# Two chained MLPs behind an attention recurrence: weight conversion as a six-stage pipeline, second MLP's weights held in SBUF

## Chip, core and metric

One core of one Trainium2 chip. The metric is the device time of one launch in microseconds, median of several runs. The trace shows one more execution, taken with the hardware profiler.

## What is computed

```python
def _attn_ref(r, k, v, w, a, b):          # each [4, 8, 768, 40], float32
    state = np.zeros((B, H, D, D))
    for t in range(S):
        y[:, :, t] = np.einsum('bhd,bhde->bhe', rt, state)
        Sa = np.einsum('bhde,bhe->bhd', state, at)
        state = state * wt[:, :, None, :] - np.einsum('bhd,bhe->bhde', Sa, bt) \
              + np.einsum('bhd,bhe->bhde', vt, kt)
    return y

x = y.transpose(0, 2, 1, 3).reshape(3072, 320)
x = np.maximum(x @ moe_w_in, 0.0) ** 2 @ moe_w_out            # [320, 2048], [2048, 320]
h = x @ moe2_w_in
out = (h * np.clip(h + 3.0, 0.0, 6.0) / 6.0) @ moe2_w_out
```

The MLP weights reach the kernel as float64. A float64 is two 32-bit words to the kernel, so each weight has to be put together as a float32 from them, and then split into a high part that TensorE's fp32r format holds exactly and a low part, the rest. Products are taken as high x high, high x low and low x high.

## The kernel before

The attention runs in 48 **slots**, one for a chunk of 64 steps of one of four batches. A slot's order is the string ORDER (ORDER0 until the first MLP has inputs), each word a step; four of its words are M. At an M the program calls `fill`, which emits one **piece** of MLP work if there is one (`Moe.piece`) or else a few matmuls that keep TensorE busy, then five steps of a triangular inverse and, with them, steps of the weight conversion (`cstep`). The scheduler is off (`manual_schedule`), so each engine runs its instructions in the order in which this code emits them.

An MLP has 16 blocks f of 128 hidden units. Tokens go in six **groups** of 512. An in-piece (`project_in`) makes a block's hidden values, an out-piece (`out1`, `out2`) adds the block to the output in PSUM. So a group is 32 pieces. A group's inputs are loaded when the attention has written them, every eight slots; the last group of the first MLP and all of the second come after the loop.

`convert` is a generator that turns weights from float64 bits into parts. A **part** is one block of w_in (384 columns) or of w_out (320), in the order two of w_in, two of w_out; 32 parts make an MLP. For each part it emits: load of the bits on SP (L94), Abs of the high word on ScalarE (L126, or L138), scaling of the low word on ScalarE (L130), mask and shift on VectorE (L127), join on VectorE (L135), add of the words on GpSimd (L139), a select that zeroes the smallest on VectorE (L146), a cast to the high part on ScalarE (L70, L74, L75), the subtraction that leaves the low part (L156, GpSimd for w_in, VectorE for w_out), and a store of the low part to DRAM (L78). `finish` holds the last four and is emitted after the next part's first steps.

High parts stay in SBUF. Low parts are read again from DRAM, two blocks at a time, whenever a group needs them (`pair`, L169, on ScalarE's DMA queue), into the rotating buffers wi and wo of the pool m_rot, or m_l2 in the second MLP. In the first MLP the first 16 parts are converted in the slots before the first group (`need(raw1, n_early)` after slot 7); from block 8 on (`direct`) a part is converted straight into the buffer from which the first group reads it, and is held until in-piece f - 2 has been emitted. In the second MLP all parts are direct and held like that, with two steps after each piece. After the loop, four loads of bits and the inputs of the second MLP's first two groups are put on SP's queue at once (L993 to L996).

Of the kernel before, what the change touches and what calls it, by code (L numbers as in the profile page):

```python
# [24 lines left out]
DM = 320  # L25
# [8 lines left out]
class Moe:  # L34


    def __init__(self, tc, ctx, pctx, consts):
# [7 lines left out]
        self.pso4, self.gpool, self.depth = None, self.rot, 2  # L45
# [3 lines left out]
        self.pairs = {}  # L49
# [4 lines left out]
    def weights(self, pool, dram, second, rot):  # L54


        w = {"second": second, "rot": rot, "in": pool.tile([128, NF, 3, 128], F32R, name="wi_hi"),
             "out": pool.tile([128, NF, DM if second else 256], F32R, name="wo_hi")}
        w["li"], w["lo"] = ([dram.tile([128, 2, 384], FP32, name=f"{n}{second}_{k}") for k in range(NF // 2)]
                            for n in ("LI", "LO"))  # L60
        return w

    def split(self, w, part, f, raw, t):

        nc = self.nc
        n = 384
        if part == 0 or w["second"]:
            n = DM if part else 384
            hi = w["out"][:, f] if part else w["in"][:, f].rearrange("p k c -> p (k c)")
            nc.scalar.copy(out=hi, in_=raw)  # L70
            self.low(t[:, 0:n], raw, hi, nc.vector if part else nc.gpsimd)
        else:
            hi = w["out"][:, f]
            nc.scalar.copy(out=hi, in_=raw[:, 0:256])  # L74
            nc.scalar.copy(out=t[:, 0:64], in_=raw[:, 256:320])  # L75
            self.low(t[:, 128:384], raw[:, 0:256], hi, nc.vector)
            self.low(t[:, 64:128], raw[:, 256:320], t[:, 0:64], nc.vector)
        (nc.sync if part else nc.gpsimd).dma_start(out=w["lo" if part else "li"][f // 2][:, f % 2, 0:n], in_=t.bitcast(FP32)[:, 0:n])  # L78

    def convert(self, w, w_in, w_out, scratch, first, direct):  # L80

        nc = self.nc
        self.raw = w
        self.converted = 0
        todo = deque()
        order = [(f, part) for q in range(0, NF, 2) for part in range(2) for f in (q, q + 1)]

        def load(k):
            f, part = order[k]
            bits = scratch(k, 0)[:, 0:640 if part else 768]
            nc.sync.dma_start(out=bits, in_=(w_out if part else w_in)[f])  # L94
            return bits.rearrange("p (c w) -> p c w", w=2)

        count = [0, 0]

        def fill():

            while count[0] < len(order) and count[0] - count[1] < scratch(count[0], 2):
                todo.append(load(count[0]))
                count[0] += 1

        fill()
        yield
        late = []
        for k, (f, part) in enumerate(order):
            n = DM if part else 384
            if f >= direct and f % 2 == 0:  # L110

                while (self.n_out if part else self.n_in) < first + f - 2:
                    if late:
                        late.pop()()
                    yield "held"
                self.pairs[w["second"], part, f] = w["rot"].tile([128, 2, 384], F32R, tag=("wi", "wo")[part], name="wd")
            own = scratch(k, 3)
            fill()
            bits = todo.popleft()
            low, high = bits[:, :, 0], bits[:, :, 1]  # L120
            t = scratch(k, 1)[:, 0:n]

            q, m = (x[:, 0:n] for x in own) if own else (low, high)
            q, m = q.bitcast(I32), m.bitcast(FP32)
            if own:
                nc.scalar.activation(out=m, in_=high.bitcast(FP32), func=ACTF.Abs)  # L126
            nc.vector.tensor_scalar(out=t, in0=high, scalar1=0x07FFFFFF, scalar2=3, op0=ALU.bitwise_and,  # L127
                                    op1=ALU.logical_shift_left)
            yield
            nc.scalar.mul(out=q, in_=low, mul=2.0 ** -29)  # L130
            yield
            if late:
                late.pop()()
                yield
            nc.vector.scalar_tensor_tensor(out=t, in0=high, scalar=0xC0000000, in1=t, op0=ALU.bitwise_and,  # L135
                                           op1=ALU.bitwise_or)
            if not own:
                nc.scalar.activation(out=m, in_=high.bitcast(FP32), func=ACTF.Abs)  # L138
            nc.gpsimd.tensor_tensor(out=q, in0=t.bitcast(I32), in1=q, op=ALU.add)  # L139
            if own:  # L140
                count[1] = k + 1
                fill()

            def finish(k=k, part=part, f=f, q=q, m=m, own=own, t=scratch(k, 1)):
                v = q.bitcast(FP32)
                nc.vector.scalar_tensor_tensor(out=v, in0=m, scalar=TINY, in1=v, op0=ALU.is_ge, op1=ALU.mult)  # L146
                self.split(w, part, f, v, self.pairs[w["second"], part, f & ~1][:, f % 2] if f >= direct else t.bitcast(F32R))
                self.converted = count[1] = k + 1

            late.append(finish)  # L150
            yield
        late.pop()()
        yield
# [4 lines left out]
    def need(self, raw, n):  # L158
        while raw is self.raw and self.converted < n:
            assert next(self.aside) != "held" or self.converted >= n  # L160

    def pair(self, w, part, f):


        t = self.pairs.pop((w["second"], part, f), None)
        if t is None:
            n = DM if part and w["second"] else 384
            t = w["rot"].tile([128, 2, 384], F32R, tag=("wi", "wo")[part], name="wl")
            self.nc.scalar.dma_start(out=t.bitcast(FP32)[:, :, 0:n], in_=w["lo" if part else "li"][f // 2][:, :, 0:n])  # L169
        return t  # L170

    def block_in(self, w, f):

        if f % 2 == 0:
# [4 lines left out]
    def block_out(self, w, f):  # L179
        if f % 2 == 0:  # L180
# [4 lines left out]
    def load_x(self, src, second):  # L185
        nc = self.nc
        t = self.xpool.tile([128, 3 + second, TOK], F32R, tag="xr", name="xr")
        xr = t.bitcast(FP32)
        nc.sync.dma_start(out=xr[:, 0:2], in_=src[0:256].rearrange("(k p) t -> p k t", p=128))
        for h in range(2):  # L190
            for s in range(1 + second):
                nc.sync.dma_start(out=xr[64 * h:64 * h + 64, 2 + s], in_=src[256 + 64 * s:320 + 64 * s])
        return t

    def split_x(self, t, second):

        nc = self.nc
        xr = t.bitcast(FP32)
        xm = self.xpool.tile([128, 2, TOK], F32R, tag="xm", name="xm")
        hi = self.rot.tile([128, TOK], F32R, tag="r", name="xh")  # L200
        if second:
            v = self.rot.tile([128, TOK], FP32, tag="g", name="xs")
            nc.vector.tensor_tensor(out=v, in0=xr[:, 2], in1=xr[:, 3], op=ALU.add)
# [10 lines left out]
    def project_in(self, w, x, second, between):  # L214
# [12 lines left out]
        gs = self.gpool.tile([128, 2, TOK], F32R, tag="gs", name="gs")  # L227
# [26 lines left out]
    def out2(self, acc, w, gs, f):  # L254
# [3 lines left out]
        for q in range(4):  # L258
            s = slice(128 * q, 128 * q + 128)
            nc.tensor.matmul(acc[q], gs[:, 0, s], hi, start=a, stop=False)  # L260
            nc.tensor.matmul(acc[q], gs[:, 0, s], lo[:, 0:DM], start=False, stop=False)  # L261
# [13 lines left out]
    def prep(self):  # L275
        g = self.loaded.popleft()
# [56 lines left out]
def general_path(tc, ctx, moe, flags, nat, raws, ident, out):  # L333
# [17 lines left out]
    with tc.If(n_good < 2 * D * NS):  # L351
# [63 lines left out]
        for second, (src, dst, w) in enumerate(((xs[0], xs[1], raws[0]), (xs[1], out, raws[1]))):  # L415
            for f in range(NF):
                if f % 2 == 0:
                    for part in range(2):
                        n = DM if part and second else 384
                        nc.sync.dma_start(out=rest[part][:, :, 0:n], in_=w["lo" if part else "li"][f // 2][:, :, 0:n])  # L420
# [4 lines left out]
                if second:  # L425
                    nc.vector.tensor_tensor(out=wo[:, f], in0=hi, in1=lo[:, 0:DM], op=ALU.add)
                else:
                    nc.vector.tensor_tensor(out=wo[:, f, 0:256], in0=hi, in1=lo[:, 128:384], op=ALU.add)
                    nc.vector.tensor_tensor(out=wo[:, f, 256:320], in0=lo[:, 0:64], in1=lo[:, 64:128], op=ALU.add)
# [23 lines left out]
def rwkv_moe_moe2_kernel(ctx, tc, pre_in, vr_in, v_in, nat, ident_d, mask_d, cst_d, w1_in, w1_out, w2_in, w2_out, out,  # L453
                         lag=8, n_early=16, depth=3, idle=4):
# [383 lines left out]
    with tc.manual_schedule():  # L838
# [12 lines left out]
        raw1 = moe.weights(wp1, dram, 0, moe.rot)  # L851
        late_scratch = []

        def scratch1(k, what):

            if what == 2:
                return 4 if k < n_early else 3
            if what == 3:
                return [moe.rot.tile([128, 384], U32, tag=x, name="cv") for x in ("g", "wo")] if k < n_early else None
            if k < n_early:  # L860
                return moe.rot.tile([128, 768 if what == 0 else 384], U32, tag="r" if what else ("wi", "gs")[k % 2],
                                    name="bits")
            if not late_scratch:
                x = moe.xpool.tile([128, 2, 768], U32, tag="xr", name="bits")
                late_scratch.append([cp.tile([128, 768], U32, name="bits"), x[:, 0], x[:, 1]])
                x = moe.xpool.tile([128, 2, 384], U32, tag="xm", name="cv_t")
# [213 lines left out]
```

## Time and profile before

| What | us |
|---|---|
| median of 3 runs (lowest, highest) | 1441.65 (1439.43, 1443.51) |
| the profiled execution's own time | 1440.75 |
| its span in the trace | 1439.0 |
| TensorE matmul busy | 1186.5 (82%) |
| VectorE busy | 792.5 (55%) |
| ScalarE busy | 610.6 (42%) |
| GpSimd busy | 409.4 (28%) |
| mean DMA rate | 124 GB/s |

A busy share is an average over the whole span.

How to read it: a busy share is a mean over stages with different limits, so it is read by stretches. The page's cut of the span in 40 slices shows the stages: up to some 430 us TensorE's digits go up and down between 3 and 9, from there to 950 they stay at 9 or near it, from 950 to 1115 they fall back to 6, and from 1115 on they are 9. GpSimd has work up to 790 and again from 970 to 1115. The chain that ended last puts 36% of the span on TensorE, 13% on VectorE, 11% on DMA.

### The profile page before, as it was taken

Reading aid. Unit: us, or ns where it says so; the run is one execution under the profiler, and the core shown is the slowest. Engines: PE = TensorE matmul, PEld = TensorE weight load, DVE = VectorE, ACT = ScalarE, POOL = GpSimd, SP = SyncE. Lnnn points to the kernel's source line nnn. Section 1 sums busy time; section 2 is a strip of 40 time slices with the busy share of each in tenths; the row PEclk is TensorE's granted clock in tenths of the full one; section 3 lists DMA queues with packets and bytes.
Section 4 is the critical chain, followed back from the end, with each engine's and each line's share of the span. In section 5 each row is a group of like instructions: output and inputs, shape, how many; then the busy total and the mean of one; then the engine's idle time right before and its main releaser. Section 6 shows DMA issues by size and latency. Waiting matters only on the chain.

```text
span 1439.0 us, 25925 instructions
## 1 busy us (share of the span) xinstructions
PE 1186.5 (82%) x9682; PEld 1003.3 (70%) x9682; DVE 792.5 (55%) x1841; ACT 610.6 (42%) x1456; POOL 409.4 (28%) x612
## 2 busy tenths in 40 slices
PE   3177787976679899999999899797666899999994
PEld 3166776855568677777778778585544798888984
DVE  7823667586575949575765733345554444344432
ACT  4144443535445445445444433344444433344331
POOL 5685454344534333333332000003333000000000
PEclk9668689987689999999999999898778999999997
DMA  5534556636537475665655442634333443434331
GB/s 127 135 79 132 124 123 141 145 94 145 131 95 164 104 143 150 138 122 137 140 133 107 128 111 76 213 110 149 121 112 99 135 130 118 138 104 136 102 118 50
DMA packets 270150, 178.43 MB, mean 124 GB/s; under 512 B 202944, under 2 KB 228160, under 8 KB 270016
## 3 DMA queue, kind: packets, MB, share of 16 engines
q1 hardware_dynamic: 238656, 106.95, 32.5%
q10 hardware_dynamic: 29312, 63.45, 14.7%
q0 software_dynamic: 2048, 6.29, 1.1%
q8 instruction: 79, 1.29, 0.4%
q14 instruction: 55, 0.45, 0.1%
HBM read 140.99 MB, written 35.65 MB: 123 GB/s over the span
## 4 chain that ended last, share of the span: by engine, by line
PE 36%; DVE 13%; DMA 11%; ACT 4%; POOL 3%; issue 3%; SPq 1%; ACTq 0%; DVEq 0%; POOLq 0%
PE h L221 7%; PE h L223 3%; PE o L261 3%; DMA DT<-TB 3%; DMA wl<-LO 3%; PE o L262 3%; DMA wl<-LI 3%; PE o L260 2%; DVE TMP L627 2%; DVE INV L630 2%; PE o L248 2%; POOL cv L139 2%; PE h L225 2%; PE h L224 2%; PE o L250 2%
## 5 line engine op out<-in xcount | busy, mean ns | idle before, releaser
L221 PE MATMUL h<-xm,wi_hi 128*128 128x512 f32 x384 | 165.9, 432 | 38.5 <-ACT wi_hi L70 38.5
L239 DVE TENSOR_TENSOR gs<-g,gs 128x512 fp32r<-128x512 f32 x192 | 143.8, 749 | 80.7 <-ACT gs L233 68.8
L221 PE MATMUL h<-xm,wl 128*128 128x512 f32 x336 | 134.5, 400 | 22.5 <-DMA wl<-LI 22.5
L627 DVE TENSOR_TENSOR TMP<-ML,INV 128x126 f32<-128x126 f32 (+22 forms) x341 | 109.7, 322 | 70.1 <-DMA ML<-DT 50.9
L596 POOL TENSOR_TENSOR RK<-RK,mask 64x256 f32<-64x256 f32 x96 | 74.0, 771 | 255.6 <-ACT RK L595 244.4
L231 DVE SCALAR_TENSOR_TENSOR g<-r,h 128x512 f32<-128x512 f32 x96 | 65.9, 686 | 124.5 <-ACT r L230 124.4
L236 DVE TENSOR_TENSOR g<-r 128x512 f32<-128x512 f32 x96 | 66.6, 694 | 112.1 <-ACT r L235 112.1
L260 PE MATMUL o<-wo_hi,gs 128*128 128x320 f32 x384 | 123.0, 320 | 4.8 <-ACT os L822 3.0
L262 PE MATMUL o<-wo_hi,gs 128*128 128x320 f32 x384 | 122.6, 319 | 1.9 <-DVE gs L239 1.9
L223 PE MATMUL h<-xr,wi_hi 128*128 128x512 f32 x384 | 123.2, 403 | 0.0
L230 ACT ACTIVATE r<-h,cst 128x512 f32<-128x512 f32 x96 | 66.0, 687 | 122.2 <-PE h L225 117.8
L139 POOL TENSOR_TENSOR cv<-bits,cv 128x384 int32<-128x384 int32 (+1 forms) x48 | 44.7, 931 | 254.2 <-DVE bits L127 183.4
L221 PEld LDWEIGHTS h<-xm,wi_hi 128*128 128x128 f32 x384 | 76.9, 200 | 49.9 <-ACT wi_hi L70 40.5
L630 DVE TENSOR_TENSOR INV<-INV,TMP 128x126 f32<-128x126 f32 (+22 forms) x341 | 106.7, 313 | 7.9
L235 ACT ACTIVATE r<-h 128x512 f32<-128x512 f32 x96 | 57.2, 596 | 104.7 <-PE h L225 95.1
L261 PE MATMUL o<-wl,gs 128*128 128x320 f32 x320 | 99.9, 312 | 0.4
L233 ACT CAST gs<-g 128x512 fp32r<-128x512 f32 x96 | 59.5, 620 | 71.7 <-DVE g L231 71.7
L221 PEld LDWEIGHTS h<-xm,wl 128*128 128x128 f32 x336 | 64.1, 191 | 34.9 <-DMA wl<-LI 26.6
L223 PEld LDWEIGHTS h<-xr,wi_hi 128*128 128x128 f32 x384 | 75.1, 196 | 17.6
L248 PE MATMUL o<-gs,wo_hi 128*128 128x512 f32 x192 | 86.9, 452 | 0.0
L557 POOL TENSOR_TENSOR RK<-IN,EE 40x256 f32<-40x256 f32 x82 | 69.8, 852 | 57.6 <-DVE EE L545 54.3
L260 PEld LDWEIGHTS o<-wo_hi,gs 128*128 128x128 f32 x384 | 74.9, 195 | 14.1 <-ACT gs L233 6.6
(174 smaller groups left out, 2763.8 us busy)
## 6 DMA issues: line engine op xcount, KB each, us to landing
wl<-LI ACTq DMA_DIRECT2D x84, 384.0 KB
IN<-in_pre_dram SPq DMA_DIRECT2D x44, 418.0 KB
wl<-LO ACTq DMA_DIRECT2D x44, 384.0 KB
wl<-LO ACTq DMA_DIRECT2D x40, 320.0 KB
bits<-in_moe_w_in_dram SPq DMA_DIRECT2D x32, 384.0 KB
bits<-in_moe_w_out_dram SPq DMA_DIRECT2D x32, 320.0 KB
VR<-in_vr_dram SPq DMA_DIRECT2D x96, 80.0 KB
DT<-TB SPq DMA_DIRECT2D x24, 256.0 KB
```

The source lines that it names most:

```text
L139: nc.gpsimd.tensor_tensor(out=q, in0=t.bitcast(I32), in1=q, op=ALU.add)
L221: nc.tensor.matmul(h, w[p][:, k], xm[:, k], start=(k + p == 0), stop=False)
L223: nc.tensor.matmul(h, hi[:, k], lo[:, k], start=False, stop=False)
L239: nc.vector.tensor_tensor(out=gs[:, 1], in0=g, in1=gs[:, 0].bitcast(FP32), op=ALU.subtract)
L248: nc.tensor.matmul(acc[d], hi, gs[:, 0], start=a, stop=False)
L260: nc.tensor.matmul(acc[q], gs[:, 0, s], hi, start=a, stop=False)
L261: nc.tensor.matmul(acc[q], gs[:, 0, s], lo[:, 0:DM], start=False, stop=False)
L262: nc.tensor.matmul(acc[q], gs[:, 1, s], hi, start=False, stop=z)
L557: e.tensor_tensor(out=rk[P, :, 64 * h:64 * h + 64], in0=a[P], in1=E[P, :, 0:64], op=ALU.mult)
L596: nc.gpsimd.tensor_tensor(out=o, in0=o, in1=mask[P].unsqueeze(1).to_broadcast([64, NP, 64]), op=ALU.mult)
L627: eng.tensor_tensor(out=tmp, in0=ml[:, s, s + 1:32].unsqueeze(2).to_broadcast([128, n, w]), in1=inv[:, s, 0:w].unsqueeze(1).to_broadcast([ ...
L630: eng.tensor_tensor(out=inv[:, s + 1:32, 0:w], in0=inv[:, s + 1:32, 0:w], in1=tmp, op=ALU.subtract)
```

## The change

The conversion of a part is cut into six stages. Stage one scales the low word (ScalarE) and masks and joins the high word (VectorE), two takes Abs (ScalarE) and adds (GpSimd), three selects (VectorE), four casts the high part (ScalarE), five subtracts, six stores. One **round** runs stage six of part r - 5, five of r - 4, and so on to stage one of part r, and begins with the load of part r + 1. 32 parts make 37 rounds, after a first step that loads part 0. Every stage works in place on four rotating buffers for bits and four for results.

In the first MLP each M has one round instead of two steps, all 32 parts go through this, and `prep` of the first group first runs what is left of it. The subtraction of w_in goes from GpSimd to VectorE, and all low parts are stored to DRAM, w_in's by SP instead of GpSimd. All groups read them back from there.

In the second MLP a piece has one round after it. Low parts get tiles of their own in SBUF (`resident`, 16 x 384 and 16 x 320 columns of float32 a partition), so `pair` is not called for it; the unsplit weights are stored to DRAM for the general path, a branch that these inputs do not take. After the loop SP has two loads of bits, and the inputs of group 0 of the second MLP are loaded only after two more in-pieces. The output ring is 3 instead of 4 deep, and the third gs buffer comes with two of the pool m_rot.

```diff
-    def convert(self, w, w_in, w_out, scratch, first, direct):
+    def convert(self, w, w_in, w_out, scratch):
...
+        def first(k):
+            low, high = views(k)
+            t = res[k] = scratch("res", k)[:, 0:n_of[order[k][1]]]
+            nc.scalar.mul(out=low.bitcast(I32), in_=low, mul=2.0 ** -29)
+            nc.vector.tensor_scalar(out=t, in0=high, scalar1=0x07FFFFFF, scalar2=3, op0=ALU.bitwise_and,
+                                    op1=ALU.logical_shift_left)
+            nc.vector.scalar_tensor_tensor(out=t, in0=high, scalar=0xC0000000, in1=t, op0=ALU.bitwise_and,
+                                           op1=ALU.bitwise_or)
+        def second(k):
+            low, high = views(k)
+            nc.scalar.activation(out=high.bitcast(FP32), in_=high.bitcast(FP32), func=ACTF.Abs)
+            nc.gpsimd.tensor_tensor(out=low.bitcast(I32), in0=res[k].bitcast(I32), in1=low.bitcast(I32), op=ALU.add)
+        def third(k):
+            nc.vector.scalar_tensor_tensor(out=res[k].bitcast(FP32), in0=high, scalar=TINY, in1=low, op0=ALU.is_ge,
+                                           op1=ALU.mult)
+        def fourth(k):
+            if w["second"]:
+                nc.sync.dma_start(out=w["full"][f][:, 384 * part:384 * part + n_of[part]], in_=v)
+            else:
+                rest[k] = scratch("rest", k).bitcast(F32R)
+                if part:
+                    nc.scalar.copy(out=rest[k][:, 0:64], in_=v[:, 256:320])
+            nc.scalar.copy(out=hi, in_=v if w["second"] or part == 0 else v[:, 0:256])
+        def fifth(k):
+            if w["second"]:
+                self.low(w["lout"][:, f] if part else w["lin"][:, f].rearrange("p k c -> p (k c)"), v, hi,
+                         nc.vector if part else nc.gpsimd)
+            elif part == 0:
+                self.low(rest[k], v, hi, nc.vector)
+            else:
+                self.low(rest[k][:, 128:384], v[:, 0:256], hi, nc.vector)
+                self.low(rest[k][:, 64:128], v[:, 256:320], rest[k][:, 0:64], nc.vector)
+        def sixth(k):
+            if not w["second"]:
+                nc.sync.dma_start(out=w["lo" if part else "li"][f // 2][:, f % 2], in_=rest.pop(k).bitcast(FP32))
+            self.converted = k + 1
+        load(0)
+        yield
+        for r in range(n + 5):
+            if r + 1 < n:
+                load(r + 1)
+            for lag, stage in ((5, sixth), (4, fifth), (3, fourth), (2, third), (1, second), (0, first)):
+                if 0 <= r - lag < n:
+                    stage(r - lag)
+            yield
...
     def block_in(self, w, f):
+        if w["second"]:
+            self.need(w, 2 * (f - f % 2) + 4)
+            return w["in"][:, f], w["lin"][:, f]
...
     def block_out(self, w, f):
+        if w["second"]:
+            return w["out"][:, f], w["lout"][:, f]
...
     def prep(self):
+        if self.raw is self.plan[0][1]:
+            for _ in self.aside:
+                pass
...
                     for k in range(5):
                         tick()
-                        if k < 2:
-                            cstep(1)
+                    cstep(1)
...
-            if i == 2 * NB - 1:
-                moe.need(raw1, n_early)
...
-        opool = hctx.enter_context(tc.tile_pool(name="m_o2", bufs=4))
+        opool = hctx.enter_context(tc.tile_pool(name="m_o2", bufs=3))
+        cv2 = hctx.enter_context(tc.tile_pool(name="m_cv2", bufs=4))
...
-        cstep(9)
+        moe.steps = 1
+        cstep(2)
         moe.loaded and moe.loaded[0].update(age=0)
-        for g in range(2):
-            moe.load(groups2[g])
         moe.early, moe.age = 8, 0
-        for g in range(2, NG + 1):
+        for g in range(NG):
             while moe.n_in < (NG + g - 1) * NF + 2:
                 moe.piece()
-            if g < NG:
-                moe.load(groups2[g])
+            moe.load(groups2[g])
```

Three places show how this moves instructions. TensorE's order stays as it is.

First, ScalarE in one of the first slots of the attention loop. In the rows cv, bits, res and rest are buffers of the conversion, a is PSUM, RHS and TB belong to the attention. Before:

```order
L126 ACTIVATE cv<-bits 128x320
L672 COPY RHS_137<-a 128x160
L130 ACTIVATE cv<-bits 128x320
L70 CAST wi_hi<-cv 128x384
L584 COPY TB_129<-a 64x256 x2
```

With the change:

```order
L122 CAST wi_hi<-res 128x384
L104 ACTIVATE bits<-bits 128x320
L96 ACTIVATE bits<-bits 128x320
L677 COPY RHS_137<-a 128x160
L122 CAST wi_hi<-res 128x384
L104 ACTIVATE bits<-bits 128x320
L96 ACTIVATE bits<-bits 128x384
L589 COPY TB_131<-a 64x256 x2
```

Between two copies of the attention there is now one conversion instruction of each of three parts, and every M has such a set.

Second, SP's queue at the end of the loop. xr are a group's inputs, X_5 the first MLP's last group, X_0 and X_1 the second MLP's first two; os are outputs, W the unsplit weights. Before:

```order
L728 DMA X_5_62<-XT_148 40x4x128 x4
L189 DMA xr<-X_5_62 128x2x512
L192 DMA xr<-X_5_62 64x512 x2
L94 DMA bits<-in_moe_w_in_dram 128x768 x2
L94 DMA bits<-in_moe_w_out_dram 128x640 x2
L189 DMA xr<-X_0_63 128x2x512
L192 DMA xr<-X_0_63 64x512 x4
L189 DMA xr<-X_1_64 128x2x512
L192 DMA xr<-X_1_64 64x512 x4
L823 DMA X_4_67<-os 128x512 x3
```

With the change:

```order
L189 DMA xr<-X_5_62 128x2x512
L192 DMA xr<-X_5_62 64x512 x2
L83 DMA bits<-in_moe_w_in_dram 128x768 x2
L83 DMA bits<-in_moe_w_out_dram 128x640 x2
L83 DMA bits<-in_moe_w_in_dram 128x768
L117 DMA W_0_215<-res 128x384
L83 DMA bits<-in_moe_w_in_dram 128x768
L117 DMA W_1_216<-res 128x384
L83 DMA bits<-in_moe_w_out_dram 128x640
L117 DMA W_0_215<-res 128x320
L189 DMA xr<-X_0_63 128x2x512
```

The inputs X_0 come behind seven loads and three stores instead of four loads, X_1 behind all of them, and each load is one round ahead of its use.

Third, ScalarE in a later group of the second MLP, where wl are low parts that are read from DRAM. Before:

```order
L230 ACTIVATE r<-h,cst 128x512
L169 DMA wl<-LI_4_9615 128x768
L233 CAST gs<-g 128x512
L169 DMA wl<-LO_3_9622 128x2x320
L230 ACTIVATE r<-h,cst 128x512
```

With the change:

```order
L231 ACTIVATE r<-h,cst 128x512
L234 CAST gs<-g 128x512
L837 COPY os<-o_12483 128x320
L837 COPY os<-o_12485 128x320
L231 ACTIVATE r<-h,cst 128x512
```

The two DMA issues for every two blocks are gone.

## Rows read from the trace of the kernel before

**Rows 1.** Busy time by engine in stretches (start:end, length), x is instructions: by windows.

```profile
core 0: us, PE busy (x) PEld busy (x) DVE busy (x) ACT busy (x) POOL busy (x), PEclk, DMA share, GB/s
71.80:247.30 175.50, 138.09 (x1496) 124.36 (x1494) 90.85 (x249) 75.66 (x225) 98.79 (x153) 0.77 0.51 118
247.30:429.70 182.40, 136.38 (x1250) 112.57 (x1248) 121.46 (x306) 86.50 (x229) 81.47 (x108) 0.81 0.52 123
...
978.40:1112.80 134.40, 86.41 (x314) 65.85 (x313) 69.60 (x140) 61.42 (x125) 50.33 (x59) 0.75 0.37 120
1112.80:1414.80 302.00, 290.65 (x1583) 257.93 (x1581) 125.89 (x191) 115.06 (x184) 0.88 (x1) 0.99 0.41 120
0.00:72.00 72.00, 20.86 (x130) 18.99 (x132) 57.78 (x151) 22.25 (x63) 42.98 (x87) 0.80 0.56 131
```

**Rows 2.** The same stretches, instructions of line 670 alone (16 a slot).

```profile
247.30:429.70 182.40, 5.47 (x128) 4.50 (x128) 0.81 0.52 123
429.70:816.90 387.20, 15.96 (x384) 13.13 (x384) 0.96 0.59 133
```

**Rows 3.** Who waited for whom from 247.3 to 429.7: total us, times, longest us.

```profile
PE a L680 <- ACT RHS L672: 28.0, 5, 6.1
ACT bits L138 <- DVE cv_t L135: 25.6, 12, 6.4
```

**Rows 4.** The same stretches, GpSimd instructions of line 139 alone (one a part).

```profile
247.30:429.70 182.40, 15.76 (x16) 0.81 0.52 123
...
978.40:1112.80 134.40, 26.95 (x29) 0.75 0.37 120
```

**Rows 5.** The chain of work that ended last, 1180 to 1270: start us, us, what.

```profile
1204.63 0.93 PE h L221 x4
...
1208.22 0.93 PE h L221 x4
...
1246.12 7.14 DMA wl<-LI
...
1264.70 0.93 PE h L221 x4
```

**Rows 6.** Groups by line and shape: xcount, busy us, mean ns, idle time before.

```profile
L139 POOL TENSOR_TENSOR cv<-bits,cv 128x384 int32<-128x384 int32 x24 | 24.0, 1000 | 200.3 <-DVE bits L127 183.4 <-ACT cv L130 15.1 <-DVE INV L630 1.5
...
L139 POOL TENSOR_TENSOR cv<-bits,cv 128x320 int32<-128x320 int32 x24 | 20.7, 861 | 53.8 <-DVE bits L135 53.6
...
L156 POOL TENSOR_TENSOR wd<-cv,wi_hi 128x384 fp32r<-128x384 f32 x16 | 16.0, 1002 | 19.9 <-ACT wi_hi L70 19.9
...
L146 DVE SCALAR_TENSOR_TENSOR cv<-cv 128x384 f32<-128x384 f32 x24 | 15.1, 629 | 39.8 <-POOL cv L139 39.8
...
L135 DVE SCALAR_TENSOR_TENSOR bits<-bits 128x384 uint32<-128x384 uint32 x24 | 13.3, 554 | 0.1
...
L146 DVE SCALAR_TENSOR_TENSOR cv<-cv 128x320 f32<-128x320 f32 x24 | 11.7, 487 | 14.3 <-POOL cv L139 14.3
...
L135 DVE SCALAR_TENSOR_TENSOR bits<-bits 128x320 uint32<-128x320 uint32 x24 | 11.6, 482 | 0.0
...
L127 DVE TENSOR_SCALAR bits<-bits 128x384 uint32<-128x384 uint32 x24 | 9.5, 396 | 7.0 <-POOL cv L139 5.8 <-DMA LO<-bits 1.2
...
L156 DVE TENSOR_TENSOR wd<-cv,wo_hi 128x320 fp32r<-128x320 f32 x16 | 7.9, 492 | 8.4 <-ACT wo_hi L70 8.4
```

**Rows 7.** Instructions in order of time: start us, us, engine, what.

```profile
1014.20 1.00 POOL L156 TENSOR_TENSOR wd<-cv,wi_hi 128x384 fp32r<-128x384 f32 x1 [1.21 <-ACT wi_hi L70]
...
1014.67 1.07 DVE L239 TENSOR_TENSOR gs<-g,gs 128x512 fp32r<-128x512 f32 x1 [1.10 <-ACT gs L233]
...
1180.95 0.69 DVE L239 TENSOR_TENSOR gs<-g,gs 128x512 fp32r<-128x512 f32 x1 [0.69 <-ACT gs L233]
```

**Rows 8.** The same view at 904, on the SP queue.

```profile
903.98 1.05 SPq L94 DMA_DIRECT2D bits<-in_moe_w_in_dram  x2
```

**Rows 9.** Who waited for whom from 900 to 978.4.

```profile
PE h L221 <- DMA wl<-LI: 10.2, 1, 10.2
```

More of the change, by code (lines that the diff above doesn't have):

```diff
@@ L52, in __init__, with weights, resident @@
         nc.sync.dma_start(out=self.cst, in_=consts["cst"])
[L54 to L59, printed above, removed]
+    def weights(self, pool, dram, rot):
+        w = {"second": 0, "rot": rot, "in": pool.tile([128, NF, 3, 128], F32R, name="wi_hi"),
+             "out": pool.tile([128, NF, 256], F32R, name="wo_hi")}
+        w["li"], w["lo"] = ([dram.tile([128, 2, 384], FP32, name=f"{n}_{k}") for k in range(NF // 2)]
                             for n in ("LI", "LO"))
         return w
[L63 to L78, printed above, removed]
-    def convert(self, w, w_in, w_out, scratch, first, direct):
+    def resident(self, w, pool):
+        for n in ("in", "lin"):
+            w[n] = pool.tile([128, NF, 3, 128], F32R, name=f"w2_{n}")
+        for n in ("out", "lout"):
+            w[n] = pool.tile([128, NF, DM], F32R, name=f"w2_{n}")
+    def convert(self, w, w_in, w_out, scratch):
         nc = self.nc
@@ L87, in convert @@
         self.converted = 0
-        todo = deque()
         order = [(f, part) for q in range(0, NF, 2) for part in range(2) for f in (q, q + 1)]
+        n_of = (384, DM)
+        bits, res, rest = {}, {}, {}
         def load(k):
             f, part = order[k]
[L93 to L126, printed above, removed]
+            bits[k] = scratch("bits", k)[:, 0:2 * n_of[part]]
@@ new lines, in load, with views, high_of @@
+            nc.sync.dma_start(out=bits[k], in_=(w_out if part else w_in)[f])
+        def views(k):
+            b = bits[k].rearrange("p (c w) -> p c w", w=2)
+            return b[:, :, 0], b[:, :, 1]
+        def high_of(k):
+            f, part = order[k]
+            return w["out"][:, f] if part else w["in"][:, f].rearrange("p k c -> p (k c)")
+        def first(k):
+            low, high = views(k)
+            t = res[k] = scratch("res", k)[:, 0:n_of[order[k][1]]]
+            nc.scalar.mul(out=low.bitcast(I32), in_=low, mul=2.0 ** -29)
@@ L139, in convert @@
[L139 to L148, printed above, removed]
@@ L151, in convert @@
             yield
-        late.pop()()
-        yield
     def low(self, o, x, hi, engine):
@@ L159, in need @@
         while raw is self.raw and self.converted < n:
-            assert next(self.aside) != "held" or self.converted >= n
+            next(self.aside)
     def pair(self, w, part, f):
[L165 to L169, printed above, removed]
+        t = w["rot"].tile([128, 2, 384], F32R, tag=("wi", "wo")[part], name="wl")
+        self.nc.scalar.dma_start(out=t.bitcast(FP32), in_=w["lo" if part else "li"][f // 2])
         return t
     def block_in(self, w, f):
+        if w["second"]:
+            self.need(w, 2 * (f - f % 2) + 4)
+            return w["in"][:, f], w["lin"][:, f]
         if f % 2 == 0:
@@ L424, in general_path @@
                 hi = w["out"][:, f].bitcast(FP32)
[L425 to L429, printed above, removed]
+                nc.vector.tensor_tensor(out=wo[:, f, 0:256], in0=hi, in1=lo[:, 128:384], op=ALU.add)
+                nc.vector.tensor_tensor(out=wo[:, f, 256:320], in0=lo[:, 0:64], in1=lo[:, 64:128], op=ALU.add)
             with tc.For_i(0, B * S, 128) as r0:
```

96 lines of the change are left out of this document (43 added, 53 removed).

## Prediction

> **What bounds the kernel now.** I read the stretches first [rows 1], then how many slots and conversions each holds, then the waits, then single instructions. All times are of the profiled execution: 1440.75 us, of which 1439.0 are span. The median of the runs shown is 1441.65, 0.9 above it, so 0.9 is added at the end. About 0.3% (4.3 us) is what a measurement of this kernel can tell from no change.
>
> [rows 1] cut the run where the kind of work changes. Matmul busy share alone does not say what a stretch is worth; the pace of its slots and pieces does. The attention loop runs 16 matmuls of line 670 per slot, so [rows 2] give 128/16 = 8 slots in the 182.4 us from 247.3 and 384/16 = 24 slots in the next 387.2 us: 22.8 us a slot against 16.1. The two stretches run the same program but for 16 weight parts that are converted in the first of them. The waits there [rows 3] show how a conversion gets into the attention path: ScalarE's Abs (L138) waits for VectorE (25.6 us in 12 waits), whatever stands behind it in ScalarE's queue waits too, and TensorE loses 28.0 us on the copy RHS.
>
> The second MLP's first group (16 in-pieces and 16 out-pieces) takes the 134.4 us from 978.4, and 29 conversions fall into it [rows 4]. Its later groups take 60.07 us from start to start [rows 5], of which 16 x 3.59 = 57.5 is matmul pace; the chain names a reload of low parts (wl<-LI) at each boundary. So both slow places are places where converting paces the products.
>
> **The change, part by part.** Durations are means of [rows 6]. A part of w_in (384 columns) costs VectorE 0.40 + 0.55 + 0.63 = 1.58 and GpSimd 1.00 + 1.00 = 2.00; a part of w_out (320) costs VectorE 0.40 + 0.48 + 0.49 + 0.49 = 1.86 and GpSimd 0.86. That is (3.58 + 2.72)/2 = 3.15 us a part on the two engines together. In the changed first MLP the w_in subtraction moves to VectorE (0.49 x 384/320 = 0.59, an estimate): (3.17 + 2.72)/2 = 2.95.
>
> The two engines have to be added because they hold each other up. In [rows 7] a VectorE subtraction that starts at 1014.67, inside a GpSimd subtraction that ends at 1015.20, takes 1.07 us, where the same one takes 0.69 at 1180.95, and ends 0.54 after it. So it got only about 0.15 us done while GpSimd ran.
>
> *First MLP's group 0, slots 10 to 17.* The 16 conversions leave. 37 rounds, one per M, begin after a first step before the loop and end in slot 9; the drain in prep then finds nothing to do. The 8 slots fall to 8 x 16.1 = 129: **-53**. Ends: -28, the wait that rows 3 name outright, and -53. I take -53, because the next 24 slots are this program without conversions.
>
> *Slots 0 to 9.* Here 16 parts become 32. VectorE and GpSimd are busy 90.85 + 98.79 = 189.6 us now, 1.08 per us of stretch (above 1 as blocked time counts as busy). Out go 16 x 3.15 = 50.4, in come 32 x 2.95 = 94.4: 233.6. At 1.08 that takes 216 us (+41). The densest long stretch, 0 to 72, has (57.78 + 42.98)/72 = 1.40; at that it takes 167 (-9). The stretch from 247.3 reaches (121.46 + 81.47)/182.4 = 1.11 even with chains of waits that the six stages loosen: every operand now comes from the round before. I take 1.20, thus 195 us: **+19**.
>
> *The end of the loop and the second MLP's first group.* Loads start at 904 [rows 8], and nearly all 37 rounds, one per piece, run beside the first MLP's last group. Two rounds carry two parts (6.30) and a product's two VectorE operations at 0.69, 7.68 in all, 3.84 a round if nothing overlaps. VectorE's share alone is 1.58 + 1.86 + 1.38 = 4.82, 2.41 a round. Nine VectorE instructions at 0.15 of overlap bring 7.68 to 6.33, 3.17 a round; I take 3.3, near that end, since each engine has a round's time before its operand is late. 37 x 3.3 = 122 ends at 1026; the second MLP's group 0 follows at pace with 60, so it ends at 1086 instead of 1112.8: **-27**. Ends: -60 (2.41) and -7 (3.84). Also gone is a 10.2 us wait for a low part [rows 9], which four weight loads and two groups of inputs on SP had delayed; it lies inside this stretch and is not counted again.
>
> *The second MLP's other five groups.* Their low parts stay in SBUF, so 80 loads leave ScalarE's queue. 302.0 us falls to 5 x 57.5 = 288: **-14**. Ends: -7 (half the boundary stays, since next in line there are the copies of the outputs) and -14.
>
> *Costed at nothing.* The low and full stores move to SP. In slots 0 to 9 that is 40 DMAs more at about half a us of issue (two took 1.05, [rows 8]), 20 us of a queue over 175; cover is the round's lead that each load has. If it fails, attention's inputs, which stand behind them in the same queue, come late. Transfers: 0.51 busy at 118 GB/s there means 231 GB/s when full, and 16 more parts at 352 + 192 KB are 8.9 MB or 39 us, which lifts the share to 0.73. In the last group, per round, 352 + 176 KB and 192 KB of reloads in 3.3 us are 0.22 MB/us against 120/0.37 = 324 GB/s when full. Both hide. ScalarE loses its waits and gains no more than it has idle. The smaller rings in the second MLP (outputs 3 instead of 4) are nothing while the pace is TensorE's.
>
> Sum: -53 + 19 - 27 - 14 = -75; 1440.75 - 75 + 0.9 = **1366 us**.
>
> [...]
>
> **The rivals.**
> 1. *Blocking is complete and nothing loosens.* A round costs 3.84 (-7) and slots 0 to 9 stay at 1.08 (+41): -53 + 41 - 7 - 14 = -33, **1408**. For it: the blocked subtraction of rows 7. Against it: 1.40 in the first 72 us.
> 2. *Blocking hardly matters.* 2.41 a round (-60) and slots at 1.40 (-9): -53 - 9 - 60 - 14 = -136, **1306**. Against it: rows 7.
> 3. *Slower: the in-order queues pass the wait on.* A part costs what it costs in the second MLP's first group now, 134.4/29 = 4.63 us. Place: slots 0 to 9, where 16 more parts add 74, and the last group, where 37 x 4.63 = 171 and 60 end at 1135, +22. -53 + 74 + 22 - 14 = +29, **1471**. It decides from 4.1 us a part in both places: 16x + 37x - 149 (the room from 904 to 1112.8 less 60) = 53 + 14. For it: VectorE, GpSimd and ScalarE still hand each part on five times, behind attention's work. Against it: now one chain of waits serves one part at a time, then five parts are under way.
> 4. *The change does not do what it says for group 0.* The slow slots have another cause and stay: 1366 + 53 = **1419**. For it: rows 3 name only 28 of the 53. Against it: nothing else differs from the slots that follow.
>
> **How the numbers follow.** Forecast 0.48, rival 1 0.24, rival 2 0.12, rival 3 0.09, rival 4 0.07. The range 1310 to 1425 holds the forecast, rivals 1 and 4 and the near part of 2, which leaves rival 3 and the far part of 2 outside, under 2 in 10. Rival 3 alone ends above; its near end, 0.01 to 0.02, lies within 0.3%. Faster 0.90, same 0.02, slower 0.08.
>
> **What would show it.** Right: 8 slots after the first in-piece at about 16 us each; no conversions in that stretch; slots 0 to 9 near 195 us; 32 pieces of the last first-MLP group at about 6.6 us a pair, then 3.59 a pair to the end with no wl loads; TensorE's clock near 1.00 from there on. [...]

## The result, and the profile after

The changed kernel takes **1397.8 us** (median, 1394.5 to 1401.8) beside 1442.6 (1439.4 to 1444.9) before: ratio 0.969, 95% interval 0.965 to 0.973. It gained 44.8 us where 75 were forecast. The profiled execution took 1400.85 us, of which 1399.1 are span, 3.0 above the median; of before, 1439.0. The stretches of the changed kernel, cut at the same kinds of work as [rows 1]; columns as there:

```profile
core 0: us, PE busy (x) PEld busy (x) DVE busy (x) ACT busy (x) POOL busy (x), PEclk, DMA share, GB/s
72.00:278.00 206.00, 154.17 (x1496) 138.54 (x1494) 144.74 (x333) 97.66 (x281) 106.40 (x154) 0.68 0.58 144
278.00:412.30 134.30, 121.56 (x1249) 100.00 (x1248) 92.43 (x240) 63.62 (x173) 51.62 (x76) 0.95 0.57 131
412.30:867.80 455.50, 425.90 (x4436) 350.26 (x4432) 287.10 (x745) 213.32 (x568) 132.38 (x202) 0.96 0.56 129
867.80:995.60 127.80, 98.48 (x455) 76.41 (x452) 102.40 (x155) 70.31 (x145) 52.70 (x44) 0.88 0.68 210
995.60:1059.80 64.20, 60.26 (x313) 52.58 (x312) 33.13 (x50) 27.55 (x47) 5.09 (x4) 0.97 0.19 56
1059.80:1399.10 339.30, 301.77 (x1620) 271.48 (x1619) 125.34 (x190) 115.21 (x184) 0.00 (x0) 0.94 0.07 23
```

The first two are slots 0 to 9 and 10 to 17, the third the loop's slots 18 to 46, the fourth its end and the first MLP's last group, the fifth the second MLP's group 0, the last its other five groups (to 1376.2) with the tail. Set against before, with the forecast's terms:

| stretch | before | after | change | forecast |
|---|---|---|---|---|
| slots 0 to 9 | 175.5 | 206.0 | +30.5 | +19 |
| slots 10 to 17 | 182.4 | 134.3 | -48.1 | -53 |
| slot 18 to the end of the second MLP's group 0 | 683.1 | 647.5 | -35.6 | -27 |
| its other five groups | 302.0 | 316.4 | **+14.4** | **-14** |
| tail, and the first 72 us | 96.0 | 94.9 | -1.1 | 0 |

The sum is -39.9, the difference of the spans. The largest miss has the wrong sign: these five groups, now without any loads of low parts, are slower than with them. Who waited for whom from 1059.8 to the end (total us, times, longest us); line 837 is the copy of an output out of its accumulator in PSUM, line 261 the first product into one:

```profile
ACT gs L234 <- DVE g L232: 84.5, 80, 5.3
DVE gs L240 <- ACT gs L234: 54.9, 80, 0.7
DVE os L837 <- DMA out_dram<-os: 31.5, 6, 5.5
PEld o L261 <- DVE os L837: 21.9, 5, 4.5
PE o L261 <- DVE os L837: 20.6, 5, 4.2
```

And one boundary between groups in order of time (start us, us, engine, what, in brackets the idle time before it), VectorE's instructions and then TensorE's:

```profile
1130.87 0.48 DVE L837 COPY os<-o 128x320 f32<-128x320 f32 x1
1136.55 0.49 DVE L837 COPY os<-o 128x320 f32<-128x320 f32 x1 [5.20 <-DMA out_dram<-os]
1136.96 0.68 DVE L232 SCALAR_TENSOR_TENSOR g<-r,h 128x512 f32<-128x512 f32 x1
...
1132.66 0.31 PE L263 MATMUL o<-w_out,gs 128*128 128x320 f32 x1
1137.10 0.63 PE L261 MATMUL o<-w_out,gs 128*128 128x320 f32 x1 [4.13 <-DVE os L837]
1137.53 0.47 PE L262 MATMUL o<-w_lout,gs 128*128 128x320 f32 x1
```

A group ends in four copies of its output, two on ScalarE and two on VectorE. With a ring of three the fourth needs the buffer of the first, whose store has just been issued, and it waits 5.2 us for that store to land. Meanwhile the accumulator it should empty stays full, so TensorE's first product into it waits 4.1 us, and the next `g` stands behind it on VectorE. Nothing of the kind shows before: there no copy waits for a store, and TensorE waits 10.0 us, in 5 waits, for reloads of low parts (such a reload is in [rows 5]).

### The profile page after: what moved, and what is told of

It is laid out like the page before. It is cut to its first block, busy times and chain, and to the rows that moved or that the text cites. A ratio compares the mean times of both kernels' runs of the same rounds, so it can differ in the third digit from the quotient of the medians.

```text
span 1399.1 us, 25891 instructions
## 1 busy us (share of the span) xinstructions
PE 1182.9 (85%) x9682; PEld 1008.2 (72%) x9682; DVE 841.3 (60%) x1857; ACT 609.9 (44%) x1456; POOL 390.7 (28%) x564
## 4 chain that ended last, share of the span: by engine, by line
PE 48%; DMA 19%; DVE 17%; SPq 4%; issue 4%; ACT 4%; POOL 3%; DVEq 0%; ACTq 0%; POOLq 0%
PE h L222 9%; DMA DT<-TB 5%; PE h L224 4%; PE o L261 4%; PE o L262 4%; PE o L263 4%; DVE INV L635 3%; DVE TMP L632 3%; DMA out_dram<-os 3%; DMA W<-res 2%; PE h L225 2%; PE h L226 2%; SPq L622 2%; PE o L249 2%; PE a L586 2%
## 5 line engine op out<-in xcount | busy, mean ns | idle before, releaser
L261 PE MATMUL o<-w_out,gs 128*128 128x320 f32 x384 | 121.0, 315 | 22.1 <-DVE os L837 20.6
L105 POOL TENSOR_TENSOR bits<-res,bits 128x384 int32<-128x384 int32 (+1 forms) x64 | 70.3, 1100 | 223.6 <-DMA wl<-LI 124.5
L262 PE MATMUL o<-w_lout,gs 128*128 128x320 f32 x384 | 120.1, 313 | 0.0
L263 PE MATMUL o<-w_out,gs 128*128 128x320 f32 x384 | 120.0, 312 | 0.0
L222 PE MATMUL h<-xm,wl 128*128 128x512 f32 x192 | 78.5, 409 | 25.4 <-DMA wl<-LI 25.4
L261 PEld LDWEIGHTS o<-w_out,gs 128*128 128x128 f32 x384 | 73.7, 192 | 28.0 <-DVE os L837 21.9
L249 PE MATMUL o<-gs,wo_hi 128*128 128x512 f32 x192 | 90.6, 472 | 2.5 <-DVE os L827 1.7
L687 ACT ACTIVATE VR<-a 40x256 f32<-40x256 f32 x96 | 36.3, 378 | 112.7 <-PE a L685 112.1
L222 PE MATMUL h<-xm,wi_hi 128*128 128x512 f32 x192 | 83.8, 437 | 1.9 <-ACT xm L208 1.9
L250 PE MATMUL o<-gs,wo_hi 128*128 128x512 f32 x192 | 82.7, 431 | 2.0 <-DVE gs L240 2.0
L251 PE MATMUL o<-gs,wl 128*128 128x512 f32 x192 | 81.9, 427 | 0.7 <-DMA wl<-LO 0.7
L577 POOL TENSOR_TENSOR KBt<-IN,RV 104x256 f32<-104x256 f32 x78 | 72.4, 948 | 32.5 <-DVE TMP L632 11.8
```

The lines of the kernel that those rows point to most:

```text
L222: nc.tensor.matmul(h, w[p][:, k], xm[:, k], start=(k + p == 0), stop=False)
L249: nc.tensor.matmul(acc[d], hi, gs[:, 0], start=a, stop=False)
L250: nc.tensor.matmul(acc[d], hi, gs[:, 1], start=False, stop=False)
L251: nc.tensor.matmul(acc[d], lo, gs[:, 0], start=False, stop=z)
L262: nc.tensor.matmul(acc[q], gs[:, 0, s], lo, start=False, stop=False)
L263: nc.tensor.matmul(acc[q], gs[:, 1, s], hi, start=False, stop=z)
```

## The experiments

**The ring of outputs, both ways.** The changed kernel with four buffers, and the kernel before with three:

```
# e1: changed kernel
-                o = opool.tile([128, DM], FP32, name="os")
+                o = moe.rot.tile([128, DM], FP32, tag=("wo", "wi")[q % 2], name="os")
# e2: kernel before
-        opool = hctx.enter_context(tc.tile_pool(name="m_o2", bufs=4))
+        opool = hctx.enter_context(tc.tile_pool(name="m_o2", bufs=3))
```

> The changed kernel with one edit: the four copies of a group's output go to four buffers that lie idle in the second MLP (two of each of two tags) instead of a ring of three. Theory (the ring is what the five later groups lose): VectorE's 5.5 us waits for the store of an output are gone, the distance from group to group falls from 64.3 to between 58.5 and 60 us, the time from the second MLP's group 1 to the end falls from 339 by 20 to 30, and the whole kernel takes 1368 to 1378. Rival (the boundary is held by TensorE's accumulators and the splitting of the next inputs, and the ring only happens to be the last name): the distance stays at 62 or more and the kernel at 1390 or more.

> The kernel before with one edit: its ring of four output buffers in the second MLP becomes three. Theory (the ring's price does not depend on the rest of the change): the distance from group to group rises from 60.1 by 2 to 4.3 us, and the kernel from 1442.6 to 1452 to 1463. Rival (the boundary there waits for a reload of low parts anyway, which covers the ring): under 0.3% change, 1438 to 1447.

Measured: e1 **1364.5** us, ratio 0.945 (0.940 to 0.950); e2 **1461.1**, ratio 1.012 (1.007 to 1.018). The five groups of e1:

```profile
1058.20:1342.00 283.80, 283.80 (x1581) 257.29 (x1580) 122.56 (x184) 113.07 (x180) 0.00 (x0) 1.00 0.08 25
```

TensorE is busy in all of it, 57.5 us from group to group: nothing but matmul pace is left. The same stretch of the changed kernel:

```profile
1059.80:1376.20 316.40, 295.80 (x1582) 266.02 (x1582) 122.64 (x184) 113.04 (x180) 0.00 (x0) 0.96 0.07 23
```

The 32.6 us between them are 20.6 of idle TensorE, the wait above, and 12.0 in which the same products took longer. After the wait shown the granted clock is 0.50 from 1137.1 to 1141.0 and 1.00 again from 1145, and the first product takes 0.63 us where one before takes 0.31; over the five groups the mean is 0.96. In e2 the same wait appears in the kernel before, and the distance from group to group goes from 60.1 to 65.1 us:

```profile
DVE os L832 <- DMA out_dram<-os: 34.8, 6, 6.0
PEld o L260 <- DVE os L832: 22.9, 5, 5.2
PE o L260 <- DVE os L832: 21.6, 5, 5.0
```

The ring's theory holds in both kernels; that the reload covers it in the one before is refuted. e1 came out a little below the theory's range, since the boundary vanished altogether, and e2's groups lost 5.0 us where up to 4.3 were expected.

**The first MLP's last group: reloads or VectorE?** In the changed kernel TensorE waits there 20.6 us, in 6 waits, for low parts. e3 takes away the stores that could delay them, e6 thins out the conversions (on top of e1).

```
# e3
-            if w["second"]:
-                nc.sync.dma_start(out=w["full"][f][:, 384 * part:384 * part + n_of[part]], in_=v)
-            else:
+            if not w["second"]:
# e6, with steps = 0.625
-        for _ in range(self.steps):
+        self.owed += self.steps
+        while self.owed >= 1:
+            self.owed -= 1
             next(self.aside, None)
```

> The changed kernel without the 32 stores of the second MLP's whole weights (W<-res); left out is what only the general path, which this input does not take, would read. Theory (those stores delay the reloads of low parts, for which TensorE waits 20.6 us in the first MLP's last group): the 94 us of that group's last sixteen in-pieces fall to 80 to 84, and the kernel takes 1383 to 1389. Rival (VectorE and GpSimd set the pace of those rounds, and the reloads would only wait in another place): 1394 to 1402.

> The version with four output buffers and one more edit: in the second conversion five rounds go to eight pieces instead of one to each, so that it reaches into the second MLP's group 0. Theory (VectorE sets the pace of the first MLP's last group, 88.3 of 94.4 us busy, and has 30 us to spare in the group that follows): the two groups together, 97 + 64 = 161 us, fall to 130 to 145, and the kernel from 1364.5 to 1333 to 1349. Rival (the pace is that of the reloads of low parts and of the loads of bits, not of work; the waits move along into the next group): 155 or more, the kernel 1358 to 1370. Slower by over 5 us if the second MLP's group 0 has to wait for its parts more than the last group gains.

Measured: e3 1394.6 us, ratio 0.966 (0.961 to 0.971), no difference from the changed kernel's 0.969 that this can tell; the group's sixteen in-pieces take 94.5 us beside 94.4 in the changed kernel, though the DMA share falls from 0.76 to 0.60, and TensorE still waits 20.0 us for reloads, in 5 waits. So the stores do not set the pace. e6 **1347.1**, 0.935 (0.930 to 0.941). The two groups in e1 and in e6:

```profile
897.00:994.30 97.30, 72.22 (x258) 55.92 (x257) 90.31 (x135) 60.22 (x124) 52.80 (x45) 0.85 0.76 235
994.30:1058.20 63.90, 60.33 (x314) 52.68 (x313) 31.30 (x48) 26.24 (x43) 3.69 (x3) 0.97 0.17 52
```

```profile
892.40:963.40 71.00, 63.17 (x258) 50.30 (x257) 62.62 (x94) 44.08 (x88) 33.58 (x27) 0.94 0.77 236
963.40:1037.10 73.70, 62.49 (x313) 53.06 (x312) 53.94 (x89) 40.21 (x79) 21.23 (x20) 0.95 0.42 127
```

VectorE was busy 90.3 of 97.3 us in the one group and 31.3 of 63.9 in the next. Shared out, the two take 144.7 in place of 161.2, and TensorE's waits for reloads come to 6.2 us, beside 20.6 in the changed kernel's last group of the first MLP. So the rounds set that group's pace, and the waits for reloads are for the most part a place where TensorE stands while the rounds are behind. e6 thins out a round's work and its loads together; that VectorE is the engine that counts is read from its 90.3 of 97.3 us and was not tested by itself.

**Slots 0 to 9: what do 32 parts cost, and by what?** Six edits, e4 on the changed kernel, the others on e1; e8 and e9 also have the edit of e5.

```
# e4, first MLP only; the scale of the low bits times 0.93
-            nc.gpsimd.tensor_tensor(out=low.bitcast(I32), in0=res[k].bitcast(I32), in1=low.bitcast(I32), op=ALU.add)
+            nc.vector.tensor_tensor(out=low, in0=res[k], in1=low, op=ALU.bitwise_or)
# e5, first MLP only, with a fifth buffer of bits
-            if r + 1 < n:
-                load(r + 1)
+            if r + lead < n:
+                load(r + lead)
...
-        moe.aside = moe.convert(raw1, w1_in.bitcast(U32), w1_out.bitcast(U32), scratch1)
+        moe.aside = moe.convert(raw1, w1_in.bitcast(U32), w1_out.bitcast(U32), scratch1, 2)
# e8
-                nc.sync.dma_start(out=w["lo" if part else "li"][f // 2][:, f % 2], in_=rest.pop(k).bitcast(FP32))
+                nc.gpsimd.dma_start(out=w["lo" if part else "li"][f // 2][:, f % 2], in_=rest.pop(k).bitcast(FP32))
# e9
+            if not w["second"] and f % 2:
+                nc.sync.dma_start(out=w["lo" if part else "li"][f // 2], in_=whole[k])
# e7: VectorE's and GpSimd's instructions of the first MLP's conversion left out; ScalarE writes the buffer that is stored
+                nc.scalar.copy(out=rest[k][:, 0:n_of[part]], in_=v)
...
# e11: its conversion left out; zeros in its place
-        moe.aside = moe.convert(raw1, w1_in.bitcast(U32), w1_out.bitcast(U32), scratch1)
+        moe.raw, moe.converted = raw1, 2 * NF
```

> The changed kernel, in the first MLP's conversion alone: GpSimd's addition (1.1 us each, 32 times) becomes a bitwise OR on VectorE, with the low bits scaled by 0.93 so that they never carry (the last bit of a weight can differ). Theory (VectorE and GpSimd hold each other up, so what counts is the sum of the two): out go 35 us of GpSimd, in come 32 operations of 0.4 to 0.55, 16 us: the sum falls by 19, and slots 0 to 9 go from 206 to about 190; the kernel takes 1380 to 1387. Rival (the two run beside each other and VectorE's in-order queue is what the slots wait for): VectorE gets 16 us more, and the kernel takes 1405 to 1414. Third (the slots wait for neither): 1394 to 1402.

> The version with four output buffers and one more edit: the first MLP's conversion loads its bits two rounds ahead instead of one (a fifth buffer holds them). Theory (slots 0 to 9 wait for late loads: in the changed kernel the chain of that stretch gives 11.4% of 206 us to loads of w_out, and ScalarE waits 54 us for them in 13 waits, with attention's work behind it in its queue): slots 0 to 9 go from 204 to 182 to 192, the kernel from 1364.5 to 1343 to 1353. Rival (the loads are late because SP's queue is, and VectorE and GpSimd have the parts to do in any case): slots 0 to 9 stay at 198 to 207, the kernel at 1358 to 1368.

> The version with four output buffers, where the first MLP's conversion keeps its loads, its stores and about its number of ScalarE's operations, and leaves out everything that VectorE and GpSimd do in it: the weights of the first MLP are not converted. Theory (late loads and SP's queue hold slots 0 to 9): they stay at 185 or more. Rival (the work of VectorE and GpSimd holds them, in queue order if not in sum): they fall to 150 to 170. The 175 us of the kernel before, with 16 parts, lie between.

> The version with four output buffers and loads two rounds ahead, and one more edit: the 32 stores of the first MLP's low parts go from SP's queue to GpSimd's. Theory (what is left of the loss in slots 0 to 9 is SP's in-order queue, in which these stores wait for VectorE while loads and attention's inputs stand behind them): slots 0 to 9 go from 193 to 175 to 187, the kernel from 1358.8 to 1341 to 1353. Rival (GpSimd then pays for issuing them, and VectorE waits for GpSimd's additions behind them): 195 to 215, the kernel 1360 to 1380. No change, 190 to 196, if the stores are late for their landing and not for their queue.

> The version with four output buffers and loads two rounds ahead, and one more edit: the low parts of two neighbouring blocks are stored together, 16 stores of 384 KB on SP in place of 32 of 192 KB. Theory (SP's queue): half of the stores' issue and waits leave it, slots 0 to 9 go from 193 to 183 to 190, the kernel from 1358.8 to 1348 to 1356. Rival (the bytes, which stay the same, or the later release of the buffer that VectorE waits for, 23.1 us in 5 waits with two loads ahead): 192 to 200, the kernel 1357 to 1366.

> The version with four output buffers, where the first MLP's conversion is left out altogether, its loads and stores too: its weights are set to zero ahead of the attention loop. It shows what slots 0 to 9 take without any conversion, beside 175 us with 16 parts (before), 204 with 32 and 184 with the loads, the stores and ScalarE's share of 32. Theory (a part has one price, whether it is the 16th or the 32nd, half of it for its transfers): 145 to 152, so 1.6 to 1.9 us a part in both kernels. Rival (the first 16 parts are free, and the loss begins past them): 165 to 175.

| | slots 0 to 9, us | kernel, us | ratio (95%) |
|---|---|---|---|
| before (16 parts) | 175.5 | 1442.6 | |
| changed | 206.0 | 1397.8 | 0.969 (0.965 to 0.973) |
| e4 OR | 199.3 | 1393.5 | 0.967 (0.962 to 0.972) |
| e1 | 204.1 | 1364.5 | 0.945 (0.940 to 0.950) |
| e5: e1, and loads two rounds ahead | 193.1 | 1358.8 | 0.942 (0.937 to 0.947) |
| e8: e5, and stores by GpSimd | 196.4 | 1358.1 | 0.943 (0.939 to 0.947) |
| e9: e5, and paired stores | 199.6 | 1362.1 | 0.946 (0.942 to 0.950) |
| e7: e1, conversion without VectorE and GpSimd | 183.8 | 1346.1 (one run) | |
| e11: e1, no conversion | 136.3 | 1302.4 (one run) | |

The stretch itself varies: with nothing changed in it, the changed kernel, e1, e3 and e6 show 206.0, 204.1, 200.1 and 202.1, mean 203.1. So e4 shows no gain that can be told from this spread; its theory, 190 us, fell. The five profiles with loads two rounds ahead (e5, e8, e9 and the two joint versions below, 195.6 and 198.0) have a mean of 196.5: some 7 us less, though the whole times of e1 and e5 overlap; e5's 193.1 lies between its two theories. Where the stores stand makes no difference that these runs can tell, so the theories of e8 and e9 fell too. The two large steps are these, e11 and then e7:

```profile
80.10:216.40 136.30, 121.67 (x1498) 110.13 (x1494) 63.49 (x186) 56.18 (x169) 62.57 (x119) 0.87 0.45 90
```

```profile
73.10:256.90 183.80, 135.70 (x1496) 122.30 (x1494) 58.53 (x186) 94.15 (x281) 61.39 (x117) 0.76 0.63 161
```

Without conversions the ten slots take 136.3 us (they start 8 us later there, behind the zeros). Both theories of e11 were too high. A part costs (203.1 - 136.3)/32 = 2.1 us in the changed kernel and, if the kernel before would also take 136.3 without conversions, (175.5 - 136.3)/16 = 2.4 in that one. e7 fell between its two theories, close to the first (183.8 where that said 185 or more): 47.5 us above e11, 19 below the changed kernel's mean. But these two are no clean prices. In e7 ScalarE writes the buffer that is stored, and so ScalarE waits for earlier stores to land, with attention's copies behind it:

```profile
ACT rest L128 <- DMA LI<-rest: 42.6, 5, 13.8
...
PE a L696 <- ACT RHS L688: 41.2, 7, 12.0
```

In the changed kernel ScalarE waits for no such store in these slots. What can be said of VectorE's and GpSimd's work comes from e4 and e8:

```profile
72.40:271.70 199.30, 144.93 (x1494) 130.29 (x1492) 141.45 (x362) 97.61 (x281) 71.61 (x121) 0.70 0.59 148
```

```profile
72.10:268.50 196.40, 141.50 (x1496) 127.80 (x1494) 153.37 (x326) 99.09 (x281) 122.78 (x185) 0.74 0.57 148
```

From the changed kernel to e4 the busy sum of the two engines falls from 251.1 to 213.1 us; from e5 to e8, where GpSimd also issues the stores, it rises from 240.1 to 276.2. The stretch goes to 199.3 from a mean of 203.1, and from 193.1 to 196.4, which is within what it varies by itself. So the sum does not set it. How the 66.8 us of 32 parts divide between the two engines' work, the transfers and the in-order queues stays open; only the 7 us of late loads are told apart.

**Together.** e10 has e1, e4, e5, e6 and e9; e12 leaves out e9 and sets the steps to 9/16.

> The paired stores, the four output buffers, the loads two rounds ahead, the OR on VectorE in the first conversion and the second conversion spread over two groups (five rounds to eight pieces), together. If the gains add: 1364.5 less 17.4 (spread), 5.7 (loads), about 4 (OR) and 3 to 10 for the paired stores, 1327 to 1335. If the edits of slots 0 to 9 remove the same wait: 1335 to 1343. Over 1347 if one spoils another.

> The four output buffers, the first conversion's loads two rounds ahead and its OR on VectorE, the second conversion spread (nine rounds to sixteen pieces, where the version before had ten), and the low parts stored one by one again. If pairing the stores cost the 3 us that its run showed, and the thinner spread gains 2 to 4 more: 1336 to 1341. If the second MLP's group 0 now waits for its parts: 1342 to 1350.

Measured: e10 1343.5 us, 0.933 (0.928 to 0.937): the edits of slots 0 to 9 hardly add (195.6 us there), as its second theory said, whose upper end it just misses. e12 **1338.8**, 0.929 (0.924 to 0.934), as its first theory said; it beats both kernels, and most of that is e1 and e6.

## Why the prediction was right and wrong

*Slots 10 to 17 (-53, measured -48.1): right.* Without conversions they run at 16.8 us instead of 22.8, near the 16.1 of the slots that follow.

*Slots 0 to 9 (+19, measured +30.5): right in sign, wrong in how it was sized.* The step was to take VectorE's and GpSimd's busy sum, 233.6, over 1.20. The ratio came out close, (144.74 + 106.40)/206 = 1.22, but the sum was 251, as packed instructions got longer:

```profile
L109 DVE SCALAR_TENSOR_TENSOR res<-bits 128x320 f32<-128x320 f32 x16 | 12.4, 775 | 0.0
...
L99 DVE SCALAR_TENSOR_TENSOR res<-bits,res 128x384 uint32<-128x384 uint32 x15 | 10.7, 713 | 0.5
...
L154 DVE TENSOR_TENSOR rest<-res,wo_hi 128x256 fp32r<-128x256 f32 x16 | 8.1, 507 | 0.0
L154 DVE TENSOR_TENSOR rest<-res,rest 128x64 fp32r<-128x64 f32 x16 | 7.9, 493 | 0.0
```

(Line, engine, shapes, count, busy us, mean ns, idle before.) The select of 320 columns (L109) takes 0.78 us where [rows 6] have 0.49, and the subtraction of a w_out part is two instructions of 0.5 each, where one of 0.49 was counted. But e4 and e8 show that the sum does not set this stretch: at 1.20 e4 would take 178 us, and it takes 199.3.

The terms "costed at nothing" were the other failure here. The transfers themselves came as estimated, 8.9 MB more, at a DMA share of 0.58 where 0.73 was worked out. The cover named for the queue, one round of lead for each load, was short, as the waits of that stretch show:

```profile
ACT bits L96 <- DMA bits<-in_moe_w_out_dram: 54.2, 13, 8.8
...
DVE res L97 <- DMA bits<-in_moe_w_out_dram: 35.3, 9, 6.9
PE a L715 <- DVE GV L696: 24.6, 7, 9.5
...
PE a L685 <- ACT RHS L677: 16.6, 5, 6.7
```

ScalarE and VectorE wait for bits, and attention's operations behind them in the same queues make TensorE wait. The text expected another consequence ("attention's inputs ... come late"), and that one hardly shows: TensorE waits 1.7 us for inputs. With two rounds of lead (e5, up to 255 us) ScalarE waits 15.0 us for bits of w_in and at most 7.6 for those of w_out, in place of 54.2, and the stretch is some 7 us shorter. That is as much of the miss as the runs tie to a cause; the rest stays open.

*The end of the loop and the second MLP's group 0 (-27, measured -35.6 with slots 18 to 46 in it): right, and too cautious.* VectorE's first conversion instruction starts at 897.1 and the last one ends at 1007.5:

```profile
897.10 0.35 DVE L97 TENSOR_SCALAR res<-bits 128x384 uint32<-128x384 uint32 x1
...
1006.99 0.48 DVE L154 TENSOR_TENSOR w_lout<-res,w_out 128x320 fp32r<-128x320 f32 x1
```

Between them lie 36 rounds (32 parts through five stages), 3.07 us each beside the 3.3 taken; the 29 of them in the 94.4 us from 901.2, where VectorE is busy for 88.3, take 3.26. The first rival's round, in which none of VectorE's and GpSimd's work overlaps, was 3.84, and the trace does not bear it out for a whole round. The rest of the gain comes from a step that put group 0 behind the last round: it begins at 995.6, 12 us before the last conversion ends, since it needs a few parts at a time.

*The other five groups (-14, measured +14.4): wrong.* The step that failed is "The smaller rings in the second MLP (outputs 3 instead of 4) are nothing while the pace is TensorE's". The paragraph on these groups knew that "next in line there are the copies of the outputs". At a boundary the pace is not TensorE's: four copies come at once, and with three buffers the fourth waits for a store. With the ring at four the stretch takes 283.8, which is matmul pace, 3.59 a product: the forecast's 288 counted 80 products where the stretch holds 79 from end to end. So with the ring left alone the term comes out, -18.2 beside -14. The whole kernel then takes 1364.5 beside the forecast 1366, but that is no proof of the other terms: +28.6 in slots 0 to 9 of e1 and -35.0 from slot 18 to group 0 miss by about as much in opposite directions, which is luck.

The first rival's 1408 lies nearest to the measured time, by a road that was not taken: neither its 3.84 a round nor its -7 came, and its +41 in slots 0 to 9 is as far from the 30.5 as the forecast's +19. The second (2.41 a round) and the third (4.63 a part, 171 us in the last group) are refuted by the 3.07 a round; in slots 0 to 9 the 16 more parts added 30.5 us, 1.9 a part. The fourth fell with slots 10 to 17.

## What to carry to other kernels

Before costing a smaller ring at nothing, count how many of its buffers are asked for at once at the stage's boundary, and how long the oldest stays taken; a store's landing is part of that time (5.2 us of waiting at the boundary shown). Where removing a large work item changes a stretch less than expected, take away everything around it too: the floor of 136 us said more than any sum of busy times. Then look at what the reduced kernel waits for, since an edit that removes work can put a wait into another queue, as e7 did (42.6 us of ScalarE's). When one engine paces a stretch and idles in the next, move its side work across the boundary before making it cheaper.

## What was unexpected of the hardware

Here a wait of TensorE came with a cost beyond its length. In the five groups, 20.6 us of waits came with 12.0 us of slower products at a granted clock of 0.96 in place of 1.00. In slots 0 to 9 TensorE is idle 14.4 us more than before (51.8 beside 37.4) and busy 16.1 us more (154.2 beside 138.1) for the same 1496 matmuls, with the granted clock at 0.68 beside 0.77; without conversions the clock is 0.87 and 1498 of them take 121.7. So about half of what that stretch lost is time that no wait names.
